# Key and query transposes of six batches moved from the tensor engine to the vector engine, with a larger feed-forward share in the first half

## The chip, the cores and the metric

The kernel runs on one core of one Trainium2 chip (trn2). The metric is the device time of one execution in microseconds, smaller is better; the kernel before was run three times and its median is given. The engines are named as the profile names them: PE is TensorE (PEld its weight loads), DVE VectorE, ACT ScalarE, POOL GpSimd, and SP the engine that issues most DMAs (SPq is its queue).

## What is computed

Top-k attention over 8 batches, 8 heads, 576 tokens and a head size of 64 is followed by a feed-forward layer with an ELU:

```python
scores = scale * np.matmul(q, k.transpose(0, 1, 3, 2))      # (8, 8, 576, 576)
kth = np.partition(scores, -32, axis=-1)[..., -32:-31]
scores = np.where(scores >= kth, scores, -1000000000.0)
attn = np.exp(scores - scores.max(-1, keepdims=True))
attn = attn / (attn.sum(-1, keepdims=True) + 1e-09)
x = np.matmul(attn, v)              # -> (4608 tokens, 512)
h = x @ w_in                        # (512, 2048)
g = np.where(h > 0.0, h, np.exp(np.minimum(h, 0.0)) - 1.0)
out = g @ w_out                     # (2048, 512)
```

The weights arrive as 64-bit floats, which the kernel turns into fp32 on the chip in its first steps. Everything else is fp32.

## The kernel before

*Steps.* The work is cut into 144 steps. Most steps are one pair of heads of one tile of 128 queries; the last 64 queries of a batch take two pairs in one step, so that a batch has 18 steps. A step goes through all engines. PE makes the scores (line 322) into PSUM, and ACT copies them out (line 342). DVE finds the 32nd largest score of each row in four rounds of MAX8 (lines 347 and 359), with three MATCH_REPLACE8 between them (line 353), for each of the two heads; these are nearly all of DVE's work. POOL turns the 32nd value into a mask (lines 371 to 373), ACT takes the exponential (line 409), PE transposes the result (line 449) and multiplies it with v (line 482). When all four pairs of a tile are through, DVE inverts the row sums (lines 418 to 420), SP sends them through DRAM to all partitions, and POOL normalises the tile (line 497).

*Feed-forward.* Normalised tiles are gathered into blocks of one to three. When the last tile of a block is normalised, the block's feed-forward is cut into pieces and put at the end of a list: 32 pieces of `hidden` (line 517, products with w_in) and 8 pieces of `project` for each tile (line 541, products with w_out). A piece has a cost in units written out by hand. In each step `feed` takes pieces off the list until a share of units is used up: the share is what is left, divided by the steps until the next block is due, but at most 6.0 in steps 0 to 71 and 7.2 after (line 580). What is still on the list after the last step is issued at the end. The list is what PE, ACT and POOL interleave with attention.

*Keys and queries.* There are 32 pairs of heads, p = 0 to 31, four a batch. For each, `load_qk` brings k and q to SBUF with tokens on the partitions, in four DMAs of 256-byte runs (one head's row of 64 values). `transpose_qk` turns them with PE: eight transposes of 128x128 (line 273) and two of the remaining 64 tokens (line 281) go to PSUM, and two ACT copies bring them to a buffer `kq` in SBUF (line 268). `keep_kq` stores it to DRAM in the next step (line 296), and `load_kq` loads it again for each step that uses it, once each odd step for the two steps that follow it, one step before their scores (line 302). The pool `kq` has five buffers, the pool `ld` for incoming k and q two.

*Order.* The order of the instructions is written out by hand, engine by engine in program order. Each engine works through its own instructions in that order, and SP also holds its DMA issues in that order, each behind the waits of the one before. Scores are made at even steps n for steps n + 2 and n + 3. The dictionary `turns` says at which step a pair is transposed: pairs 8 to 12 at steps 7 to 11, pair 13 at step 13, and from there every second step, up to pair 31 at step 49. This stands in the step behind the scores and ahead of the first MAX8, and `load_next` issues the loads of the next pair directly behind it. The functions that are touched, and the main loop that calls them, are these:

Of the kernel before, what the change touches and what calls it, by code (L numbers as in the profile page):

```python
# [61 lines left out]
def kernel(  # L62
# [150 lines left out]
    def load_qk(b, hp):  # L213

        first = b == 0 and hp < 2
        aside = (b, hp) in ((0, 1), (0, 2))
        if aside:
            home = xtpool.tile([P, 2, NC * T // 2], FP32, tag="xT", name="kqin")
            home = home[:, :, 0 : (J + 1) * 2 * D].rearrange(
                "p n (j h d) -> p n j h d", j=J + 1, h=2  # L220
            )
        for n, (name, src) in enumerate((("k", k), ("q", q))):
            queue = nc.scalar if first and name == "q" else nc.sync
            if aside:
                t = home[:, n]
            else:
                t = ldpool.tile([P, J + 1, 2, D], FP32, tag="in", name=name + "in")
            queue.dma_start(
                t[:, 0:J, :, :],
                src[b, 2 * hp : 2 * hp + 2, 0:JP, :].rearrange(  # L230
                    "h (p j) d -> p j h d", j=J
                ),
            )
            queue.dma_start(
                t[0:R, J, :, :],
                src[b, 2 * hp : 2 * hp + 2, JP:S, :].rearrange("h p d -> p h d"),
            )
            loaded[b, hp, name] = t

    def load_v(b, hp):  # L240

# [16 lines left out]
    def transpose_qk(b, hp, shared=False):  # L258

        t = kqT[b, hp] = kqpool.tile([P, 2, S], FP32, tag="kq", name="kq")  # L260
        src = [loaded.pop((b, hp, name)) for name in "kq"]

        def copy(at, ps):
            if shared:
                nc.scalar.copy(t[:, 0, at], ps[:, 0])
                nc.vector.tensor_copy(t[:, 1, at], ps[:, 1])
            else:
                nc.scalar.copy(t[:, :, at], ps)

        ps = ps_x.tile([P, 2, JP], FP32, tag="x", name="qkps")  # L270
        for n in range(2):
            for c in range(J):
                nc.tensor.transpose(  # L273
                    ps[:, n, c * P : (c + 1) * P],
                    src[n][:, c, :, :].rearrange("p h d -> p (h d)"),
                    ident[:],
                )
        copy(slice(0, JP), ps[:])
        ps = ps_x.tile([P, 2, JP], FP32, tag="x", name="qkps")
        for n in range(2):  # L280
            nc.tensor.transpose(
                ps[:, n, 0:R],
                src[n][0:R, J, :, :].rearrange("p h d -> p (h d)"),
                ident[0:R, 0:R],
            )
        copy(slice(JP, S), ps[:, :, 0:R])
# [287 lines left out]
    def feed(n, part):  # L574

        left = sum(piece[0] for piece in ffn)
        until = next(r for r in dues if r > n) - n
        share = min(left / until, 6.0 if n < NS // 2 else 7.2)  # L580

        work = 0.0
        for blk in order:
            mine = [piece[0] for piece in ffn if piece[3] is blk]
            work += sum(mine)
            late = work - 1.75 * 8 * blk.n
            if mine and late > 0 and blk.over is not None:
                share = max(share, late / max(blk.over.filled - n, 0.5))
        owed[0] = min(owed[0] + part * share, 8.0)
        while ffn and owed[0] > ffn[0][0] / 2 and ffn[0][2] < decoded[0]:  # L590
            t, piece = ffn.pop(0)[:2]
            piece()
            owed[0] -= t
# [37 lines left out]
    def sums(u):  # L631
        u.summed = True
        invert(u.g)
# [3 lines left out]
        if place in ((2, 3, 4, 5, 6) if n in (4, 5) else (3, 4, 5, 6)):  # L637
            weight_slot()

    todo, turns = {}, {}  # L640

    def at(step, fn, *args):
        todo.setdefault(step, []).append((fn, args))
# [2 lines left out]


    for p, pair in enumerate(pairs):
        if p >= NHP:
            n = p - 2 if p < NHP + 4 else p - 1  # L650
            n = n if n < EARLY + 5 else EARLY + 5 + 2 * (n - EARLY - 5)
            turns[n] = pair
            at(n + 1, keep_kq, *pair)
        elif p >= 2:
            at(p - 1, keep_kq, *pair)

# [13 lines left out]

    with tc.manual_schedule():
        load_qk(0, 0)
        nc.scalar.activation(rec[:], rec[:], AF.Copy)
        for hp in (1, 2):
            load_qk(0, hp)
        load_weights(3)
        warm(16)
        for hp in range(2):
            transpose_qk(0, hp, shared=hp == 0)
            steps[hp].kq = {hp: kqT[0, hp]}  # L680
            scores(steps[hp], 0)
            scores(steps[hp], 1, nc.vector.tensor_copy if hp == 0 else nc.scalar.copy)
            if hp == 0:
                load_qk(0, 3)
        load_weights()
        load_v(0, 0)
        first_max(steps[0])
        weight_slot()
        weight_slot()
        for hp in range(2):  # L690
            keep_kq(0, hp)
        for n in range(NS + 4):
            early = n < EARLY
            now, last, done = (
                steps[n + d] if 0 <= n + d < NS else None for d in (0, -1, -2)
            )
            for fn, args in todo.pop(n, []):
                fn(*args)
            gone = None
            if early:  # L700
                if n + 2 < NHP:
                    transpose_qk(0, n + 2)
                ahead = steps[n + 2]
                ahead.kq = {hp: kqT[0, hp] for hp in ahead.hps}
                for half in range(2):
                    scores(ahead, half)
                if n < EARLY - 1:
                    warm(24)
            elif n % 2 == 0:

                for d in (2, 3):
                    if n + d < NS:
                        for half in range(2):
                            scores(steps[n + d], half)
                    if d == 2:
                        for u in steps[n - 4 : n - 2]:
                            if not u.attended:
                                attend(u)
                                gone = u
            if n in turns and not early:  # L720
                transpose_qk(*turns[n])
                load_next()
            if now and n > 0:
                first_max(now)
            if last and n > EARLY:
                biases(last, early)
                mask(last, 0)
            if early:
                decode(n, 0)
                feed(n, 0.5)  # L730
                if last:
                    exp(last, 0)
                    exp(last, 1)
                next_max(now, (n, 1))
                decode(n, 2)
                if last:
                    trans(last)
                feed(n, 0.5)
                if last and last.ends:
                    sums(last)  # L740
                next_max(now, (n, 3))
                decode(n, 4)
                if last:
                    attend(last)
                if n in turns:
                    transpose_qk(*turns[n])
                if n < EARLY - 1:
                    warm(24)
                next_max(now, (n, 5))
                if last and last.ends:  # L750
                    normalise(last.g)
                mask_early(now)
                decode(n, 6)
                if n >= NHP - 3:
                    load_next()
                continue
            decode(n, 0)
            feed(n, (0.3, 0.7)[n % 2])
            if now:
                next_max(now, (n, 1))  # L760
            decode(n, 2)
            if last:
                if n > EARLY:
                    mask(last, 1)
                exp(last, 0)
            if done and not done.turned:
                trans(done)
            if now:
                next_max(now, (n, 3))
            decode(n, 4)  # L770
            if gone and gone.ends:
                normalise(gone.g)
            feed(n, (0.3, 0.7)[n % 2])
            if now:
                next_max(now, (n, 5))
            decode(n, 6)
            if last:
                exp(last, 1)
            if done and done.ends and not done.summed:
                sums(done)  # L780
        while ffn:
            ffn.pop(0)[1]()

# [32 lines left out]
```

## Time and profile before

| | |
|---|---|
| median of three runs | 1659.16 us (1658.2 to 1660.7) |
| the profiled execution's own time | 1660.85 us |
| its span in the profile | 1659.0 us |
| PE busy | 1593.8 us (96%) |
| DVE busy | 1460.3 us (88%) |
| POOL busy | 1141.9 us (69%) |
| ACT busy | 925.5 us (56%) |
| DMA: moved, mean rate | 174.53 MB, 105 GB/s |

The profile is one execution as the chip's profiler recorded it. The span is the time from the first to the last instruction on record; the execution's own time is a little longer. The page cuts the span into 40 slices and gives the busy tenths of each engine in each; a table of stretches gives the busy microseconds of each engine in any stretch of the span. A row of the groups has: line, engine, operation, what it writes and reads, shapes and count, then the total busy time, the mean duration of one in nanoseconds, and the idle time of the engine just ahead of it. A duration runs from the start of an instruction to its end, and neighbours on an engine overlap, so that the distance between starts can be shorter.

### The profile page before, as it was taken

The numbers are of one execution on the slowest core, as the hardware profiler recorded it, in microseconds if no ns is written. First come the engines' busy times: TensorE is split into PE (matmuls) and PEld (weight loads), VectorE is DVE, ScalarE is ACT, GpSimd is POOL, SyncE is SP. The second block draws the span as 40 slices with busy tenths as digits, with TensorE's granted clock in tenths as the row PEclk, the third lists the DMA queues.
The fourth block names the chain that finished last, engine by engine and source line by source line (L and its number), as shares of the span: only waits on it lengthen the run. The fifth ranks groups of instructions, "written<-read, shape, count | busy, mean of one in ns | idle before, by whom it ended". The sixth has DMA issues, their size and how long they took to land.

```text
span 1659.0 us, 28820 instructions
## 1 busy us (share of the span) xinstructions
PE 1593.8 (96%) x10048; PEld 1074.0 (65%) x10048; DVE 1460.3 (88%) x3074; ACT 925.5 (56%) x1889; POOL 1141.9 (69%) x1456
## 2 busy tenths in 40 slices
PE   6868999999999999999999999999999999999999
PEld 5765877777776776757566566566565566566565
DVE  6999999999999999999999989979989989987000
ACT  5875565656666565646466475466466466455121
POOL 3677777777777786868678678668668668668021
PEclk8879999999999999999999999999999999999999
DMA  9864555444543513121212321221212322210000
GB/s 304 266 184 120 185 186 152 141 132 134 162 141 97 187 52 104 65 88 67 85 71 102 116 83 61 77 85 65 91 70 100 113 68 82 77 42 7 26 7 13
DMA packets 138962, 174.53 MB, mean 105 GB/s; under 512 B 94272, under 2 KB 102464, under 8 KB 138816
## 3 DMA queue, kind: packets, MB, share of 16 engines
q1 hardware_dynamic: 136448, 172.09, 32.3%
q8 instruction: 80, 1.31, 0.3%
q10 hardware_dynamic: 2368, 0.59, 0.2%
q14 instruction: 66, 0.54, 0.1%
HBM read 144.18 MB, written 28.46 MB: 104 GB/s over the span
## 4 chain that ended last, share of the span: by engine, by line
PE 59%; DVE 26%; POOL 5%; issue 4%; DMA 3%; ACT 2%; SPq 1%; POOLq 0%; ACTq 0%
PE ops L541 21%; PE hps L517 19%; DVE m L359 11%; DVE wk L353 11%; PE avps L482 6%; PE scps L322 6%; PE eps L449 4%; DVE m L347 2%; POOL sc L373 1%; POOL gT L534 1%; DMA kin<-in_k_dram 1%; DMA w_out<-in_moe_w_in_dram 1%; POOL wk L371 1%; PE qkps L273 1%; POOL wk L372 1%
## 5 line engine op out<-in xcount | busy, mean ns | idle before, releaser
L359 DVE MAX8 m<-wk 128x8 f32<-128x576 f32 x864 | 609.8, 748 | 0.0
L517 PE MATMUL hps<-xT,w_in 128*128 128x128 f32 (+2 forms) x2432 | 534.6, 375 | 10.4 <-ACT gT L532 5.7
L541 PE MATMUL ops<-w_out,gT 128*128 128x512 f32 x1152 | 519.6, 597 | 7.6 <-ACT osb L550 7.6
L517 PEld LDWEIGHTS hps<-xT,w_in 128*128 128x128 f32 x2432 | 385.0, 194 | 134.8 <-issue 18.5
L353 DVE MATCH_REPLACE8 wk<-m,wk 128x576 f32<-128x576 f32 x576 | 423.6, 744 | 0.0
L373 POOL TENSOR_TENSOR sc<-sc,wk 128x576 f32<-128x576 f32 x276 | 389.2, 1410 | 23.0
L541 PEld LDWEIGHTS ops<-w_out,gT 128*128 128x128 f32 x1152 | 209.9, 190 | 240.2 <-issue 214.2
L409 ACT ACTIVATE sc<-sc,neg 128x576 f32<-128x576 f32 x288 | 224.1, 778 | 229.6 <-POOL sc L373 228.8
L534 POOL TENSOR_TENSOR gT<-gT,n 128x384 f32<-128x384 f32 (+1 forms) x168 | 187.2, 1121 | 189.7 <-ACT n L533 187.0
L371 POOL TENSOR_SCALAR wk<-sc,nth 128x576 f32<-128x576 f32 x276 | 206.2, 747 | 26.9
L353 DVE MATCH_REPLACE8 wk<-m,sc 128x576 f32<-128x576 f32 x288 | 211.8, 744 | 0.0
L342 ACT COPY sc<-scps 128x576 f32<-128x576 f32 x287 | 168.9, 639 | 75.6 <-PE scps L322 73.6
L322 PE MATMUL scps<-kq 64*128 64x288 f32 (+3 forms) x1344 | 181.3, 419 | 23.7 <-ACT sc L342 9.9
L347 DVE MAX8 m<-sc 128x8 f32<-128x576 f32 x288 | 201.3, 741 | 0.3
L372 POOL TENSOR_SCALAR wk<-wk 128x576 f32<-128x576 f32 x276 | 184.0, 667 | 22.8
L454 ACT COPY et<-eps 128x1024 f32<-128x1024 f32 x144 | 144.5, 1004 | 96.3 <-PE eps L449 95.3
L482 PE MATMUL avps<-et,vE 128*64 128x128 f32 (+1 forms) x3200 | 176.3, 265 | 5.6 <-ACT et L454 3.3
L482 PEld LDWEIGHTS avps<-et,vE 128*64 128x64 f32 x3200 | 158.7, 137 | 32.1 <-issue 24.7
L449 PEld LDWEIGHTS eps<-ident,sc 128*128 128x128 f32 x1152 | 134.1, 141 | 54.2 <-issue 36.6
L322 PEld LDWEIGHTS scps<-kq 64*128 64x128 f32 (+1 forms) x1344 | 101.5, 175 | 93.3 <-issue 31.2
L449 PE MATMUL eps<-ident,sc 128*128 128x128 f32 x1152 | 151.1, 274 | 7.3 <-ACT sc L409 4.6
L531 ACT ACTIVATE n<-hps 128x384 f32<-128x384 f32 (+1 forms) x168 | 90.2, 537 | 114.0 <-PE hps L517 105.4
(71 smaller groups left out, 1001.3 us busy)
## 6 DMA issues: line engine op xcount, KB each, us to landing
kq<-kqd SPq DMA_DIRECT2D x152, 576.0 KB
kqd<-kq SPq DMA_DIRECT2D x32, 576.0 KB
rb<-recd SPq DMA_DIRECT2D x64, 128.0 KB
out_dram<-osb SPq DMA_DIRECT2D x32, 256.0 KB
kin<-in_k_dram SPq DMA_DIRECT2D x30, 256.0 KB
qin<-in_q_dram SPq DMA_DIRECT2D x29, 256.0 KB
w_out<-in_moe_w_in_dram SPq DMA_DIRECT2D x2, 2048.0 KB
vE<-in_v_dram SPq DMA_DIRECT2D x32, 128.0 KB
```

The source lines that it names most:

```text
L322: nc.tensor.matmul(ps[rows, j, at : at + keys.stop - keys.start], u.kq[hp][r, 1, q0 : q0 + g.ql], u.kq[hp][r, 0, keys], start=True, stop=True,
L347: nc.vector.max(u.m1[:, i, :], u.sc[:, i, :])
L353: nc.vector.match_replace(u.wk[:, i, :], u.m[:, i, :], u.cur[:, i, :], TAKEN)
L359: nc.vector.max(u.m[:, i, :], u.cur[:, i, :])
L371: nc.gpsimd.tensor_scalar(pen, s, u.nth[:, i : i + 1], 2.0**100, ALU.add, ALU.mult)
L373: nc.gpsimd.tensor_tensor(s, s, pen, ALU.add)
L409: nc.scalar.activation(s, s, AF.Exp, bias=u.neg[:, i : i + 1], scale=scale, accum_out=g.den[:, at : at + 1],)
L449: nc.tensor.transpose(ps[:, i, c * P : (c + 1) * P], e[:, k0 + c * P : k0 + (c + 1) * P], ident[:],)
L482: nc.tensor.matmul(g.av[r, hp, 0:ql], vE[g.b, hp][:, i, (c + i) % (J + 1), :], u.et[:, at, q0 : q0 + ql], start=(c == 0), stop=(c == J),)
L517: nc.tensor.matmul(ps[:, f % G, :], w_in[:, i, f * P : (f + 1) * P], blk.xT[:, i, 0:N], start=(i == 0), stop=(i == NC - 1),)
L534: nc.gpsimd.tensor_tensor(g, g, n, ALU.subtract)
L541: nc.tensor.matmul(blk.o[:], blk.gT[f // NG][:, f % NG, s * P : (s + 1) * P], w_out[:, f, :], start=(f == 0), stop=(f == NF - 1),)
```

## The change

Pairs 0 to 7 (batches 0 and 1) stay as they are. For pairs 8 to 31 (batches 2 to 7) k and q are no longer loaded with tokens on the partitions. `load_blocks` loads each of them in eight DMAs, four for the first 512 tokens and four for the last 64, one for each group of 32 partitions: the group holds one half (32 values) of one head's row, and the runs are 128 bytes. The tokens are laid out so that, when each block of 32 partitions by 32 columns is transposed where it stands, the result is the layout of `kq`. `transpose_blocks` does that with one DVE instruction for k and one for q, each over 128 partitions and 576 columns, from the load buffer straight into `kq`.

The places move as well. A pair is transposed at the end of its step, at steps 13, 17, 21 and so on, every fourth step up to 105; k is loaded from the start of three steps ahead, q from the start of two steps ahead, and `keep_kq` follows one step behind. The call of `transpose_qk` and `load_next` in the later steps is gone. The upper limit of the share in steps 0 to 71 is 6.6 instead of 6.0.

```diff
--- before.py
+++ after.py
@@ -236,6 +236,32 @@
                 src[b, 2 * hp : 2 * hp + 2, JP:S, :].rearrange("h p d -> p h d"),
             )
             loaded[b, hp, name] = t
+
+    def load_blocks(b, hp, name):
+        t = ldpool.tile([P, J + 1, 2, D], FP32, tag="in", name=name + "bl")
+        t = t[:].rearrange("p j h d -> p (j h d)")[:, 0:S]
+        main = t[:, 0:JP].rearrange("p (c g d) -> p c g d", c=J, d=32)
+        rem = t[:, JP:S].rearrange("p (g d) -> p g d", d=32)
+        for part in range(4):
+            rows = slice(32 * part, 32 * part + 32)
+            h, d0 = 2 * hp + part // 2, part % 2 * 32
+            src = (k if name == "k" else q)[b, h, :, d0 : d0 + 32]
+            nc.sync.dma_start(
+                main[rows], src[0:JP].rearrange("(g i c) d -> i c g d", i=32, c=J)
+            )
+            nc.sync.dma_start(
+                rem[rows], src[JP:S].rearrange("(g i) d -> i g d", i=32)
+            )
+        loaded[b, hp, name] = t
+
+    def transpose_blocks(b, hp):
+        t = kqT[b, hp] = kqpool.tile([P, 2, S], FP32, tag="kq", name="kq")
+        for n, name in enumerate("kq"):
+            nc.vector.transpose(t[:, n, :], loaded.pop((b, hp, name)))
 
     def load_v(b, hp):
 
@@ -577,7 +603,7 @@
 
         left = sum(piece[0] for piece in ffn)
         until = next(r for r in dues if r > n) - n
-        share = min(left / until, 6.0 if n < NS // 2 else 7.2)
+        share = min(left / until, 6.6 if n < NS // 2 else 7.2)
 
         work = 0.0
         for blk in order:
@@ -637,7 +663,7 @@
         if place in ((2, 3, 4, 5, 6) if n in (4, 5) else (3, 4, 5, 6)):
             weight_slot()
 
-    todo, turns = {}, {}
+    todo, turns, blocks_at = {}, {}, {}
 
     def at(step, fn, *args):
         todo.setdefault(step, []).append((fn, args))
@@ -646,11 +672,15 @@
 
 
     for p, pair in enumerate(pairs):
-        if p >= NHP:
-            n = p - 2 if p < NHP + 4 else p - 1
-            n = n if n < EARLY + 5 else EARLY + 5 + 2 * (n - EARLY - 5)
-            turns[n] = pair
+        if p >= 2 * NHP:
+            n = EARLY + 7 + 4 * (p - 2 * NHP)
+            blocks_at[n] = pair
+            at(n - 3, load_blocks, *pair, "k")
+            at(n - 2, load_blocks, *pair, "q")
             at(n + 1, keep_kq, *pair)
+        elif p >= NHP:
+            turns[p - 2] = pair
+            at(p - 1, keep_kq, *pair)
         elif p >= 2:
             at(p - 1, keep_kq, *pair)
 
@@ -717,9 +747,6 @@
                             if not u.attended:
                                 attend(u)
                                 gone = u
-            if n in turns and not early:
-                transpose_qk(*turns[n])
-                load_next()
             if now and n > 0:
                 first_max(now)
             if last and n > EARLY:
@@ -778,6 +805,8 @@
                 exp(last, 1)
             if done and done.ends and not done.summed:
                 sums(done)
+            if n in blocks_at:
+                transpose_blocks(*blocks_at[n])
         while ffn:
             ffn.pop(0)[1]()
 
```

## Prediction

> **What bounds the kernel now.** I read the sliced rows of the page first: who is full, and where does it change?
>
> ```profile
> PE   6868999999999999999999999999999999999999
> DVE  6999999999999999999999989979989989987000
> ```
>
> PE and DVE are both full for most of the span, and DVE falls silent for the last three slices. So there are stages. I cut the span at the first MAX8 of a step on line 347 (144 steps, numbered from 0): step 12 starts at 186.7 us, step 72 at 780.1, step 84 at 901.4, the last DVE work ends at 1544.8. Busy time in these stretches (columns: PE, PEld, DVE, ACT, POOL, clock, DMA share, GB/s):
>
> ```profile
> 186.70:780.10 593.40, 581.63 (x4242) 427.36 (x4241) 592.08 (x1258) 356.52 (x714) 451.49 (x580) 1.00 0.39 122
> 780.10:901.40 121.30, 121.30 (x678) 76.31 (x677) 118.08 (x250) 73.47 (x157) 96.03 (x125) 1.00 0.25 87
> 901.40:1544.80 643.40, 633.10 (x3664) 381.75 (x3663) 580.60 (x1231) 352.10 (x756) 460.19 (x597) 1.00 0.22 74
> 1544.80:1659.00 114.20, 108.70 (x411) 67.61 (x409) 0.00 (x0) 22.14 (x41) 16.47 (x13) 0.99 0.04 14
> ```
>
> Steps 12 to 71: DVE idles 1.3 us of 593, 9.89 us a step; PE idles 12. DVE sets the pace, with PE just behind it. From step 84 on PE sets it: DVE idles 63 us of 643. The last 114 us are PE alone, on feed-forward left over. So time added on DVE before step 72 is paid in full, and PE work taken out from behind step 72 is gained in full.
>
> Who ends DVE's waits (waiter, releaser: total us, times, longest):
>
> ```profile
> DVE wk L353 <- POOL sc L373: 46.2, 16, 7.6
> PE scps L322 <- ACT kq L268: 7.6, 4, 5.1
> ```
>
> DVE waits for POOL's mask, which stands in POOL's queue among feed-forward results that come from PE: PE's lateness seen through POOL. The costs come from these groups:
>
> ```profile
> L359 DVE MAX8 m<-wk 128x8 f32<-128x576 f32 x864 | 609.8, 748 | 0.0
> L420 DVE STREAM_TRANSPOSE recT<-rec 128x32 f32<-128x32 f32 x40 | 8.5, 212 | 1.4
> ```
>
> and from a look at PE in one step (start, us, what):
>
> ```profile
> 440.26 0.66 PE L273 MATMUL qkps<-ident,kin 128*128 128x128 f32 x4
> ...
> 441.55 0.71 PE L517 MATMUL hps<-xT,w_in 128*128 128x128 f32 x4
> 442.09 3.60 PE L541 MATMUL ops<-w_out,gT 128*128 128x512 f32 x8
> 445.53 1.04 PE L449 MATMUL eps<-ident,sc 128*128 128x128 f32 x8
> ```
>
> One pair's ten transposes hold PE from 440.26 to 441.55, 1.29 us. Eight records of a 512-column product hold it from 442.09 to 445.53; the trace has two records for each fp32 product of the program (1152 for 576), so a product takes 0.86 us and one column 1.68 ns.
>
> [...]
>
> **The change, part by part.**
>
> *Transposes on DVE.* The built program has 48 new ones of 128x576, two a pair, at the end of steps 13, 17, ... 105. [...] neighbours overlap (MAX8 lasts 748 but starts every 660)[...]. Lower bound 0.66 (a MAX8's pace; a gain is excluded, DVE loses no work). [...] I take 0.69. Fifteen pairs (13 to 69) lie where DVE sets the pace: 30 x 0.69 = +20.7 us. The nine from 73 to 105 lie where DVE has idle time: 18 x 0.69 = 12.4 us against 18 us that DVE idles in steps 72 to 107. Their cover is thin; see the idle term.
>
> *Waits it adds.* Each transpose waits for eight DMAs, the first also for PE to be done with its kq buffer. Behind it on DVE stands the whole next step. The last block of q is issued from step n-2 on, so 28 us before use; loads issued shortly before use now land in time (PE waited 2.9 us in all for kin). I take 0; a late load costs its lateness, 0 to 3 us a pair.
>
> *Transposes off PE.* 240 transposes go, 24 x 1.29 = 31 us of PE, all of them in steps 7 to 49, where DVE sets the pace: worth nothing there by themselves. They make the room for the next part. The 24 pairs of ACT copies go too: ACT is 56% busy, nothing.
>
> *Share 6.6.* I followed the feed arithmetic through both programs and counted feed-forward columns. Steps 0 to 11: 20,992 before, 21,760 after. Steps 12 to 71: 200,192 and 215,808. Steps 72 to 147: 312,320 and 308,736. Emitted after the loop: 56,320 and 43,520. So 16,384 columns leave the part behind step 72: x 1.68 ns = -27.5 us. They go where PE then has: PE was busy 581.6 us in these 60 steps; less 19 pairs (24.5) and plus 15,616 columns (26.2) it is 583, 9.7 us a step against 10.2 of DVE. DVE is hiding them; were it not, PE would pay the 27.5 back.
>
> *The stall at step 12.* DVE waits 3.1 us at 188.1 us, at the end of a stretch where PE transposes a pair nearly each step. Five of these go (-6.5 us of PE) and 768 columns come (+1.3). I count -3.1; 0 is the other end.
>
> *New idle time of PE behind step 72.* Two sources. First, steps 72 to 107 (780 to 1154 us) held 371 us of PE and 356 of DVE; less 2048 columns (3.4) and plus 12.4 both stand at 368, so that PE runs out when it has a light step. Second, the store of pieces is thin: when block 12 becomes ready, 26.2 us of older pieces stood ahead of it, now 1.8 (blocks 11 to 16 alike, 1.8 to 3.5). PE comes to the new block about a step after its normalisation is emitted, and may wait for xT; at such thin stores in the early blocks it waited 4.7 us in two times. I take +4, from 0 to 15.
>
> *SP's queue.* 384 block issues take the place of 96; an issue of a k/q load held SP 0.62 to 0.71 us. Eight for q stand in front of the kq loads that PE's scores need one step later: 5.6 us. Where kq was issued 3.3 us before the scores PE did not wait, so it may come late by a few us; PE then lags, and the lag makes the next one on time. Nothing while DVE sets the pace; in the idle term's range otherwise.
>
> Sum against the profiled execution: 1659.0 + 20.7 - 27.5 - 3.1 + 4 = 1653.1 us of span. That execution took 1660.85, 1.85 more than its span, and lay 1.69 over the median of 1659.16. So 1653.1 + 1.85 - 1.69 = 1653.3.
>
> **The rivals.**
>
> *PE starves behind step 72* (no change). Thin stores, late kq loads and DVE's nine late pairs cost 12 us instead of 4: 1661.3. For it: six blocks with 2 us of store each. Against: PE lags DVE by some us in that stage, so that its inputs are ready.
>
> [...]
>
> *Blocks land late* (slower). Short runs and a blocked SP hold DVE at the transpose: 1 us a pair over 15 pairs is +15, 1668.3. It turns the sign from 0.4 us a pair. Against: 28 us of lead.
>
> *The change doesn't do what it says*: the columns do not move. The counts come from the built program, so I give it nothing.
>
> **How the numbers follow.** 0.2% is 3.3 us, about what a measurement of this kernel can tell from no change: faster is below 1655.8, slower above 1662.5. Forecast case 0.55 (its own range 1646 to 1657); PE starves 0.25; [...] late blocks 0.10. Faster is 0.55, the forecast case; no change 0.25, the starved one; slower 0.20. The low end takes 0.66 each (-0.9), no new idle (-4) and 2 us of lighter start: 1646. The high end reaches past the starved case with its full 15 us (1664) and the late blocks at 1668, to 1670[...].
>
> **What would show it.** Right: a wide transpose every 0.69 us; steps 13 to 71 near 10.2 us with DVE idle near 0; PE idle there up from 12 to some 28 us; DVE's end near 1560 and the part of PE alone some 20 us shorter. Wrong: [...] DVE waits for in_k or in_q ahead of them; PE waits for xT, kq or hps piling up behind step 72; the gap at 188 us still there.

## The result, and the profile after

The changed kernel takes 1698.4 us (median of four runs, 1697.29 to 1703.92) where the kernel before takes 1658.68 beside it: a ratio of 1.0246, 95% interval 1.022 to 1.0272. It is 40 us slower; the forecast was 1653.3, with a range of 1646 to 1670.

The same rows of the page as before, with the granted clock of PE below them:

```profile
PE   7867989989979989999889999999999999999999
...
DVE  7999999999979999999979998999999989989300
...
PEclk9988989999989999999999999999999999999999
```

PE has now 7s and 8s over the first half, where it had 9s, the clock drops in single slices, and DVE has single slices of 7 and 8 between its 9s. The last stretch of PE alone is shorter: two slices are empty of DVE instead of three.

Busy time by stage (columns: PE, PEld, DVE, ACT, POOL, clock, DMA share, GB/s), steps 12 to 71, 72 to 83, 84 to the last DVE work, and PE alone:

```profile
173.10:811.20 638.10, 588.61 (x4132) 428.28 (x4133) 613.72 (x1282) 340.36 (x685) 454.31 (x581) 0.97 0.37 110
811.20:943.60 132.40, 125.38 (x662) 77.03 (x659) 121.53 (x256) 69.95 (x149) 92.17 (x119) 0.96 0.32 97
943.60:1591.20 647.60, 631.74 (x3664) 380.84 (x3664) 602.25 (x1267) 356.49 (x763) 468.06 (x609) 1.00 0.28 87
1591.20:1695.50 104.30, 99.47 (x431) 65.07 (x429) 0.00 (x0) 23.32 (x43) 16.45 (x13) 1.00 0.05 15
```

In the first row both engines that could set the pace have room: DVE idles 24 us of 638, PE 49. Neither is the bound any more; they wait for each other, or both for a third. These are the waits that grew or are new:

```profile
DVE wk L379 <- POOL sc L399: 64.7, 22, 10.4
...
PE scps L348 <- DMA kq<-kqd: 51.5, 15, 9.0
...
PE hps L543 <- POOL xT L523: 8.7, 3, 6.5
```

PE waits 51.5 us, up to 9 at a time, for the loads of kq, a wait that the kernel before did not have at all. The transposes themselves are as priced, 0.68 us from start to start against the 0.69 taken:

```profile
L264 DVE STREAM_TRANSPOSE kq<-kbl 128x576 f32<-128x576 f32 x24 | 18.7, 779 | 4.6 <-issue 3.1 <-DMA recd<-recT 1.1 <-PE hps L543 0.2
...
L264 DVE STREAM_TRANSPOSE kq<-qbl 128x576 f32<-128x576 f32 x24 | 17.7, 736 | 0.0
```

Where the time went, by stage (a step starts with its first MAX8; microseconds on the profile's clock):

| stage | before | after | difference | two loads each (below) |
|---|---|---|---|---|
| up to step 12 | 175.5 | 173.1 | -2.4 | 175.6 |
| steps 12 to 71 | 593.4 | 638.1 | +44.7 | 618.3 |
| steps 72 to 107 | 373.6 | 392.6 | +19.0 | 377.1 |
| step 108 to DVE's end | 391.1 | 387.3 | -3.8 | 387.6 |
| PE alone | 125.3 | 104.3 | -21.0 | 104.3 |
| span | 1659.0 | 1695.5 | +36.5 | 1662.9 |

The span differs by 36.5 us where the medians differ by 40: of the kernel before a slower execution was profiled, of the changed kernel a faster one.

(In the prediction I had set the step times 11.2 us too late against the profile's clock: its first stretch should have begun at 175.5. The lengths of its first three stretches hold, but what lies in them shifts. Cut rightly, DVE idles 4.4 us of steps 12 to 71, not 1.3, since its wait of 3.1 us in step 12 falls inside; behind step 84 it idles 52 us, not 63; and PE works alone for 125.3 us, not 114.2. Which engine sets the pace in which stage stays the same, and no term of the sum changes.)

How a late kq load becomes a hold of DVE is seen in one place. SP's queue first (start, us, what):

```profile
448.31 1.55 SPq L450 DMA_DIRECT2D recd<-recT  x4
450.86 1.14 SPq L462 DMA_DIRECT2D rb<-recd  x2
452.09 0.54 SPq L322 DMA_DIRECT2D kqd<-kq  x1
452.68 0.62 SPq L252 DMA_DIRECT2D kbl<-in_k_dram  x1
...
458.49 0.78 SPq L277 DMA_DIRECT2D vE<-in_v_dram  x1
...
464.91 0.52 SPq L579 DMA_DIRECT2D out_dram<-osb  x1
465.79 0.64 SPq L252 DMA_DIRECT2D qbl<-in_q_dram  x1
...
471.07 2.04 SPq L328 DMA_DIRECT2D kq<-kqd  x4
```

From the moment recT lets it go, SP issues for 25 us with one pause of 1 us: the sums, eight blocks of k, ten pieces of v, an output, eight blocks of q, and only then kq. Sixteen of these 38 issues take the place of the four that a pair took before, and they hold SP for 10.3 us here. SP is not short of time on the whole: all its issues hold it for 286 us of the 638 of steps 12 to 71 (207 of 593 in the kernel before). But it waits in its order for recT, and what stands behind that wait comes in one burst. For the whole kernel that wait is

```profile
SPq L450 <- DVE recT L446: 535.9, 36, 37.9
```

Then the other engines:

```profile
475.01 2.29 PE L348 MATMUL scps<-kq 64*128 64x288 f32 x8 [8.98 <-DMA kq<-kqd]
...
486.17 1.27 POOL L560 TENSOR_TENSOR gT<-gT,n 128x512 f32<-128x512 f32 x1 [13.46 <-ACT n L559]
...
489.12 1.40 POOL L399 TENSOR_TENSOR sc<-sc,wk 128x576 f32<-128x576 f32 x1
...
490.55 0.09 DVE L379 MATCH_VALUE_LOAD wk<-m,sc 128x8 f32 x1 [10.45 <-POOL sc L399]
```

PE stands 8.98 us before the scores. From the issue of kq (471.07) to the scores (475.01) it took 3.9 us, so the issue came late, not the transfer. The scores themselves would not be missed for two steps, but PE's queue has a feed-forward piece behind them; POOL waits 13.46 us for that piece with the mask behind it, and DVE waits 10.45 us for the mask. The whole delay reaches DVE. And PE comes back at a lower clock (third row: 0.71, and in the row before 0.78, against 1.00):

```profile
455.00:465.00 10.00, 8.89 (x46) 7.88 (x46) 10.00 (x22) 4.85 (x11) 6.14 (x8) 1.00 0.39 85
465.00:475.00 10.00, 1.03 (x5) 0.59 (x4) 10.00 (x22) 2.40 (x6) 6.65 (x9) 0.78 0.56 153
475.00:485.00 10.00, 9.99 (x71) 8.12 (x72) 5.10 (x10) 2.97 (x6) 0.00 (x0) 0.71 0.36 148
485.00:495.00 10.00, 10.00 (x54) 8.92 (x53) 4.45 (x11) 6.28 (x15) 8.31 (x10) 1.00 0.01 2
```

### The profile page after: what moved, and what is told of

Read it like the earlier page. It is cut to its first block, busy times and chain, and to the rows that moved or that the text cites. A ratio compares the mean times of both kernels' runs of the same rounds, so it can differ in the third digit from the quotient of the medians.

```text
span 1695.5 us, 28732 instructions
## 1 busy us (share of the span) xinstructions
PE 1577.0 (93%) x9808; PEld 1057.2 (62%) x9808; DVE 1498.0 (88%) x3122; ACT 900.5 (53%) x1841; POOL 1141.0 (67%) x1456
## 4 chain that ended last, share of the span: by engine, by line
PE 50%; DVE 25%; POOL 7%; SPq 6%; issue 5%; DMA 4%; ACT 4%; DVEq 0%; POOLq 0%; ACTq 0%
PE ops L567 17%; PE hps L543 16%; DVE wk L379 10%; DVE m L385 10%; PE avps L508 7%; PE scps L348 6%; PE eps L475 4%; SPq L255 2%; DMA kq<-kqd 2%; SPq L252 2%; POOL sc L399 2%; DVE m L373 2%; POOL gT L560 2%; POOL wk L397 1%; POOL wk L398 1%
## 5 line engine op out<-in xcount | busy, mean ns | idle before, releaser
L348 PE MATMUL scps<-kq 64*128 64x288 f32 (+3 forms) x1344 | 191.0, 434 | 74.8 <-DMA kq<-kqd 51.5
L348 PEld LDWEIGHTS scps<-kq 64*128 64x128 f32 (+1 forms) x1344 | 106.9, 181 | 148.0 <-issue 77.1
L508 PE MATMUL avps<-et,vE 128*64 128x128 f32 (+1 forms) x3200 | 184.4, 273 | 5.6 <-ACT et L480 2.3
L508 PEld LDWEIGHTS avps<-et,vE 128*64 128x64 f32 x3200 | 166.8, 142 | 34.0 <-issue 26.1
L475 PEld LDWEIGHTS eps<-ident,sc 128*128 128x128 f32 x1152 | 133.2, 141 | 57.6 <-issue 36.5
```

The lines of the kernel that those rows point to most:

```text
L348: nc.tensor.matmul(ps[rows, j, at : at + keys.stop - keys.start], u.kq[hp][r, 1, q0 : q0 + g.ql], u.kq[hp][r, 0, keys], start=True, stop=True,
L475: nc.tensor.transpose(ps[:, i, c * P : (c + 1) * P], e[:, k0 + c * P : k0 + (c + 1) * P], ident[:],)
L508: nc.tensor.matmul(g.av[r, hp, 0:ql], vE[g.b, hp][:, i, (c + i) % (J + 1), :], u.et[:, at, q0 : q0 + ql], start=(c == 0), stop=(c == J),)
```

## The experiments

The theory, A: the time that SP needs to issue 384 block loads makes the kq loads late. The rivals: B, the share 6.6 leaves too thin a store of feed-forward pieces; C, the DVE transposes cost more than their own time; D, runs of 128 bytes are slow. Ratios are to the kernel before on the same chip, with 95% intervals.

**The share, alone and undone.** The changed kernel with 6.0, and the kernel before with 6.6.

```diff
-        share = min(left / until, 6.6 if n < NS // 2 else 7.2)
+        share = min(left / until, 6.0 if n < NS // 2 else 7.2)
```

> The changed kernel with the share of steps 0 to 71 back at 6.0; transposes and loads as changed. Theory A (SP's queue: sixteen block loads a pair stand in front of the kq loads, PE waits for kq, DVE is held later): PE still waits about 50 us for kq, and the 27.5 us of feed-forward go back behind step 72, while PE has more room to catch up; 1690 to 1710 us. Theory B (the thin store of feed-forward pieces starves PE): the store is thick again and PE's idle time behind step 72 falls back to about 12 us; 1659 + 21 for the transposes = about 1680 us.

Measured 1719.29 us, 1.0367 (1.0347 to 1.0386). PE still waits for kq, 64.7 us, and steps 12 to 71 take 638.7 us where they took 638.1: the thin store is not what holds them. B as the main cause falls; the time lies above A's range too. The share is worth 21 us to the changed kernel.

> The kernel before with the share 6.6 alone; PE still transposes. Theory A: nothing in the share itself hurts; PE, which idled 12 us in steps 12 to 71, is filled there (608 us of work in 593), those steps last about 15 us longer and the end part is 27.5 us shorter; about 1647 us. Theory B: the thin store costs 10 to 20 us of PE idle time behind step 72; 1660 to 1670 us.

Measured 1655.27 us, 0.9981 (0.9973 to 0.999): faster, but by 3 us and not by 12. Steps 12 to 71 took 611.4 us, 18 more (15 were expected), PE alone 21 less, and 2 us were lost in steps 72 to 107. So the share is a small gain by itself; a part of it is lost again where PE reaches a block before it is normalised (PE waited 6.9 us for xT in three times, 4.7 in two before).

**Fewer issues.** In the changed kernel k and q of a pair come in two DMAs each. This kernel leaves out the layout that the transposes need; it is there for its time.

```diff
-        for part in range(4):
-            ...
-            nc.sync.dma_start(main[rows], src[0:JP].rearrange(...))
-            nc.sync.dma_start(rem[rows], src[JP:S].rearrange(...))
+        src = (k if name == "k" else q)[b, 2 * hp : 2 * hp + 2]
+        nc.sync.dma_start(t[:, 0:JP]..., src[:, 0:JP].rearrange("h (p j) d -> p j h d", j=J))
+        nc.sync.dma_start(t[:, JP:S], src[0, JP - R : S])
```

> The changed kernel, but each of k and q comes in two DMAs with 256-byte runs instead of eight with 128-byte runs, in the layout of the kernel before; the blocks that DVE transposes then don't fall in place and the scores are of mixed values, all instructions but the loads are the same. Theory A: 96 issues instead of 384, the wait for kq falls from 51 us to under 10 us, DVE's holds shrink; about 1655 us. Theory C (the DVE transposes cost more than their own time): about 1690 us, since they stay. Theory B: also about 1690 us.

Measured 1661.52 us, 1.0017 (1.0008 to 1.0027). The wait for kq is down to

```profile
PE scps L344 <- DMA kq<-kqd: 4.5, 4, 3.1
```

and 37 of the 40 us are gone, with all 48 transposes in place: C falls as the main cause. The last column of the table above has its stages. It remains 8 us over the prediction's 1653.3.

**Issues against runs.** The last kernel changed two things, the number of issues and the length of the runs. So two more, each with one of them: eight issues with runs of 256 bytes, and two issues with runs of 128. Only the new lines are shown; they stand in place of the loads.

```diff
+        for part in range(4):
+            rows = slice(32 * part, 32 * part + 32)
+            nc.sync.dma_start(t[rows, 0:JP]..., src[:, 128 * part : 128 * part + 128].rearrange("h (p j) d -> p j h d", j=J))
+            nc.sync.dma_start(t[rows, JP:S], src[0, 32 * part : 32 * part + 32])
```

> The kernel with two loads each, its loads cut into eight of 32 partitions, still with 256-byte runs and the same bytes (mixed scores as there). Theory A (issue time on SP): as the changed kernel, 1690 to 1702 us. Rival D (short runs): as with two loads, 1661 us.

Measured 1697.73 us, 1.023 (1.0209 to 1.0251).

```profile
PE scps L346 <- DMA kq<-kqd: 54.0, 18, 9.4
```

```diff
+        src = (k if name == "k" else q)[b].rearrange("h s d -> (h s) d")[:, 0:32]
+        nc.sync.dma_start(t[:, 0:JP]..., src[0 : 16 * P].rearrange("(p r) d -> p r d", r=16))
+        nc.sync.dma_start(t[:, JP:S]..., src[16 * P : 18 * P].rearrange("(p r) d -> p r d", r=2))
```

> The kernel with two loads each, its loads in 128-byte runs as in the changed kernel (half of each of 2304 rows, 2304 packets a tensor; the values are of other rows and the scores are mixed). Theory A: as with two loads, 1660 to 1665 us. Rival D: near the changed kernel, 1690 us or more.

Measured 1663.8 us, 1.0031 (1.0019 to 1.0043).

```profile
PE scps L346 <- DMA kq<-kqd: 8.1, 5, 2.8
```

| | runs of 256 bytes | runs of 128 bytes |
|---|---|---|
| 2 issues a tensor | 1661.5 | 1663.8 |
| 8 issues a tensor | 1697.7 | 1698.4 |

The number of issues is worth 35 us, the length of the runs 1 to 2, which the intervals don't tell from nothing. D falls.

**The issues by themselves.** The kernel before, with 16 small DMAs a pair at the places of the blocks.

```diff
+    def idle_loads(b, hp, name):
+        t = scr.tile([P, 64], FP32, tag="scr", name="scr")
+        for part in range(4):
+            ...
+            nc.sync.dma_start(t[rows, 0:32], src[0:32, 0:32])
+            nc.sync.dma_start(t[rows, 32:64], src[JP : JP + 32, 0:32])
...
+            at(n - 3, idle_loads, *pair, "k")
+            at(n - 2, idle_loads, *pair, "q")
```

> The kernel before, with 16 more DMA issues at the places where the changed kernel loads the blocks of a pair (8 at n-3, 8 at n-2, n = 13, 17, ... 105), each of a 32x32 piece into a buffer that nobody reads; 384 issues, hardly any bytes, PE and DVE keep their work. Theory A (time that SP needs to issue): PE waits for kq for some 50 us in all as in the changed kernel, and PE has no room there; 1680 to 1700 us. Rival D (it is the short runs and their bytes, or the DVE's own part): no more than 1662 us.

Measured 1689.37 us, 1.018 (1.016 to 1.0199): 31 us for 384 issues that move 1.6 MB in all. They hold SP for 177 us. The wait for kq was 19.0 us, not 50, so a part of the loss is elsewhere: PE was also at half its clock for 26 us of steps 12 to 107, where the kernel before never was. How the loss divides between them is not shown. It lies in the same stages, +23 us in steps 12 to 71 and +7 in 72 to 107.

**The transposes by themselves.** The kernel before, with DVE transposes added.

```diff
+            if 13 <= n <= 105 and n % 4 == 1:
+                for _ in range(4):
+                    nc.vector.transpose(turned[:], w_in[:, 0, 0:288])
```

> The kernel before, with DVE transposes alone added at the places of the change: four of 128x288 at the end of steps 13, 17, ... 105, of a weight into a buffer that nobody reads; PE, loads and share as before. By the prediction's pricing 0.36 us each: 60 of them before step 72 are paid in full, 21.6 us, and those after lie in DVE's idle time; 1681 us, up to 1686 if they make PE wait there. Rival (a transpose holds DVE or POOL longer than its own time): 1695 us or more.

Measured 1685.83 us, 1.0159 (1.0142 to 1.0176).

```profile
L785 DVE STREAM_TRANSPOSE turned<-w_in 128x288 f32<-128x288 f32 x96 | 44.9, 468 | 2.5
```

All four write one buffer; they start 0.475 us apart, not the 0.36 of my estimate, and so, at 468 ns each, hardly overlap. Whether the one buffer is the reason was not tried. The 60 in steps 13 to 69 make 28.5 us, and steps 12 to 71 took 25.5 us longer, steps 72 to 107 only 1.9. DVE time is paid once where DVE sets the pace, and nearly nothing where PE does, as the prediction had it.

**Order on SP.** The kq loads of a step issued ahead of its blocks; then, besides, q's blocks one step later (n - 1 in the last line of the diff).

```diff
-            at(n - 3, load_blocks, *pair, "k")
-            at(n - 2, load_blocks, *pair, "q")
...
     for u in steps[EARLY + 2 :]:
         at(u.n // 2 * 2 - 3, load_kq, u)
+    for n, pair in blocks_at.items():
+        at(n - 3, load_blocks, *pair, "k")
+        at(n - 2, load_blocks, *pair, "q")
```

> The changed kernel with the kq loads of a step issued ahead of its block loads; nothing else. Theory A: kq is issued 5.3 us earlier in each step that loads q, so that the waits of up to 9 us shrink to about 3 to 4 us and most of the small ones go; 1665 to 1680 us. Theories B and C: no change, 1690 to 1700 us.

Measured 1668.34 us, 1.0057 (1.0035 to 1.0079). PE's wait for kq fell from 51.5 to 10.0 us, in six times, none over 3.1. Thirty of the 40 us go with nothing but an order, and the transposes, their loads and the share stay: A.

> The changed kernel with kq loads ahead of block loads, and q's blocks loaded at n-1 (an even step, in which no kq is loaded) instead of n-2. Theory A: no step has both a block load and a kq load, PE's wait for kq goes to nearly 0 and PE's clock no longer falls; about 1660 us, near the kernel with two loads each (1661.5). If the two-load kernel was better for its longer runs: like kq first, 1668 us.

Measured 1672.45 us, 1.0081 (1.0066 to 1.0096): not better, 4 us more, though the intervals touch. The wait for kq was 20.7 us in seven times. In front of the late kq loads stand, in two of the seven (7.6 us), q's blocks and pieces of v, and in the other five k's blocks and pieces of v; SP reached them late in its turn. A step of distance in the program is no distance in a queue that is behind.

**Another queue.** The blocks issued by ACT.

```diff
-            nc.sync.dma_start(main[rows], ...)
-            nc.sync.dma_start(rem[rows], ...)
+            nc.scalar.dma_start(main[rows], ...)
+            nc.scalar.dma_start(rem[rows], ...)
```

> The changed kernel with its 384 block loads issued by ACT instead of SP; layout, steps and order else as changed. Theory A: SP is free again, PE's wait for kq goes; ACT, busy 53%, takes 16 issues of 0.6 us in 40 us, but its queue now waits with the loads for DVE's transposes of the pair before; 1660 to 1670 us. If the wait for kq came from the DMA engines and not from SP's queue: 1690 us or more.

Measured 1869.76 us, 1.1264 (1.1235 to 1.1293), a clear miss. The wait for kq is gone, but each issue holds ACT itself, 388 for 233 us in all, and ACT's copies of the scores stand behind them, on which PE waits. Besides, ACT pauses between the issues of one tensor, 125 us in all, mostly until transfers of SP have landed by the trace; on SP the changed kernel has 1.4 us of such pauses. And half of the k loads, 12 of 24, begin only when DVE has ended the transposes of the pair before. So the 171 us over the changed kernel are not the price of the issues alone. The first of these waits and PE's:

```profile
ACT sc L368 <- DMA kbl<-in_k_dram: 178.6, 22, 12.3
...
PE scps L348 <- ACT sc L368: 155.7, 26, 11.6
```

**What is left of the 8 us.** The two-load kernel with the share 6.0.

> The kernel with two loads each (1661.5; blocks don't fall in place there, the scores are of mixed values) with the share back at 6.0. With SP out of the way this shows what the share is worth to the changed kernel. The prediction's sum: the 27.5 us come back behind step 72, less the 4 us it priced for the thin store, so 1685 us. If the thin store costs what the two-load kernel lies over the forecast (8 us more): 1677 us.

Measured 1678.26 us, 1.0115 (1.0098 to 1.0132). Its steps 12 to 71 took 610.8 us, 17.4 over the kernel before; with 6.6 they take 618.3. So the larger share costs the two-load kernel 7.5 us there, and is worth 17 us in all instead of 23.5. With 6.6 these steps have two waits of DVE for the mask, 3.3 us in step 13 and 5.0 in step 41; with 6.0 the longest is 0.9. Those two are about the 7.5 us. Waits in steps 12 to 71 of the two-load kernel with 6.6:

```profile
DVE wk L375 <- POOL sc L395: 8.2, 2, 5.0
PE hps L539 <- POOL xT L519: 2.6, 1, 2.6
```

PE's wait for xT grows from 8.8 us in two times to 16.6 in four, but only 2.6 us of that lie in these steps.

**A version.** Only the pairs of batches 6 and 7 go by DVE, at steps 77 to 105; the rest by PE as before, with kq ahead of blocks, q's blocks at n - 1 as in the last kernel of "Order on SP", and the share 6.6.

```diff
-        if p >= 2 * NHP:
+        if p >= 6 * NHP:
             n = EARLY + 7 + 4 * (p - 2 * NHP)
             blocks_at[n] = pair
-            at(n - 3, load_blocks, *pair, "k")
-            at(n - 2, load_blocks, *pair, "q")
             ...
         elif p >= NHP:
-            turns[p - 2] = pair
+            n = p - 2 if p < NHP + 4 else p - 1
+            n = n if n < EARLY + 5 else EARLY + 5 + 2 * (n - EARLY - 5)
+            turns[n] = pair
...
+    for n, pair in blocks_at.items():
+        at(n - 3, load_blocks, *pair, "k")
+        at(n - 1, load_blocks, *pair, "q")
...
+            if n in turns and not early:
+                transpose_qk(*turns[n])
+                load_next()
```

> A version: only the pairs of batches 6 and 7 go by DVE (steps 77 to 105), the rest by PE as before; kq loads ahead of block loads; share 6.6. DVE idled 18 us in steps 72 to 107 before and gets 11 us there; PE gets 10.3 us less than with share 6.6 alone (1655.3). Theory A: about 1646 us. If the issues hold PE in this stage too, where every us of PE counts, or PE's store of pieces is empty when it has room: 1655 to 1660 us.

Measured 1648.06 us, 0.9935 (0.992 to 0.995): faster than both kernels, and 7 us faster than the share alone. PE's wait for kq does not appear. Against the share alone the gain lies in steps 12 to 71, 601.6 us instead of 611.4: there PE sets the pace with 6.6, and the eight pairs that it no longer turns would stand in steps 35 to 49. Steps 72 to 107, where DVE turns them, take 1.4 us longer.

## Why the prediction was wrong

- **Price of a transpose: right.** 0.69 us was taken, my estimate: the kernel before has no transpose of this size on record. The starts are 702 and 659 ns apart, 0.68 us in the mean. The 30 before step 72 would have eaten the 26.6 us of the other terms (27.5 + 3.1 - 4) only from 0.89 us each on.
- **DVE's added time is paid in full before step 72: right.** 17.6 us were forecast for steps 12 to 71 (20.7 less the stall). With SP relieved and the share 6.0 it was 17.4: DVE worked 19.4 us more and waited 2.0 less. With transposes alone it was 25.5 of 28.5.
- **Columns taken from behind step 72: right for those after the loop.** PE alone lasts 21.0 us less (12,800 columns x 1.68 ns = 21.5). The other 3,584 columns, 6.0 us of the forecast 27.5, should have shortened steps 72 to the end of DVE. In the two-load kernel these steps last as long as before (+3.6 and -3.6), and PE idles 5.9 us more in them: the columns went, and new idle time took their place.
- **Waits for the blocks at the transpose: right.** DVE idled 4.6 us before all of them; "blocks land late" is out.
- **The stall at step 12: gone, with another in its place.** It was counted as gone, -3.1. In the changed kernel DVE does not wait in step 12, but 3.1 us in step 13. All nine kernels here with the share 6.6 have a wait of 2.1 to 3.3 us in step 13, and none of the five with 6.0 has; so it comes with the larger share. Nor was 3.1 a firm price: the kernel before with transposes added, the same program up to the end of step 13, waits 0.8 us in step 12.
- **New idle time of PE behind step 72: near; the share's price before it: left out.** 4 us were taken behind step 72, and the two-load kernel has 5.9. But the larger share also costs 7.5 us in steps 12 to 71 (two-load kernel with 6.6 against 6.0), where the prediction had no such term but DVE hiding the columns. What makes the two waits of DVE there is open. It is not the waits for xT alone, of which 2.6 us lie in these steps. The one in step 41 follows a wait of PE for kq of 3.1 us; with 6.0 PE waits 6.5 us for kq in step 39, and DVE loses nothing.
- **SP's queue: the step that failed.** The prediction saw the issues ("Eight for q stand in front of the kq loads that PE's scores need one step later: 5.6 us") and let them cost "Nothing while DVE sets the pace". They cost 35 us, in the profiles 20 in steps 12 to 71 and 15 in steps 72 to 107. Two things were wrong in it. It looked at the eight issues of q alone, at the distance seen in a quiet step; in the place shown above kq was issued 23 us after recT had let the queue go, with k's blocks and the loads of v in front as well. And it took a lag of PE for free while DVE sets the pace. What counted was what else waits on PE: the feed-forward piece behind the scores, and the mask behind that piece on POOL. Nor did "the lag makes the next one on time" hold: PE waited for kq in 15 places.

The sum by stage, on the profiled spans:

| stage | forecast | two loads each | changed kernel |
|---|---|---|---|
| up to step 12 | 0 | +0.1 | -2.4 |
| steps 12 to 71 | +17.6 | +24.8 | +44.7 |
| behind step 72 | -23.5 | -21.0 | -5.8 |
| span | 1653.1 | 1662.9 | 1695.5 |

With few issues the forecast misses by 9.8 us, 7.2 of them in steps 12 to 71; the profiled execution of that kernel was the slowest of its eleven, 3 us over its median. The rest, 32.6 us here and 35 to 37 in the medians, is the issues.

Not settled: how much of the 35 us is the wait itself and how much is PE's lower clock behind it. The clock was at one half for 51 us in steps 12 to 107 of the changed kernel, not once there in the kernel before, and for 20 us with two loads. No kernel took one without the other. The low clock by itself need not cost DVE anything: the two-load kernel with the share 6.0 was at half clock for 41 us of these steps, and its DVE idled only 2.4 us in steps 12 to 71. Not tried either: the sums in another place on SP, so that its queue doesn't stand behind recT.

## What to carry to other kernels

Each DMA issue held the queue it stood in, 0.62 us in the median for 8 KB of a block and 0.38 for the 576 KB of kq: count the issues of each step, add up the queue, and look for what the queue itself waits on, since what stood behind that wait came in one burst, 38 issues in 25 us; only then ask how long the bytes take. Where a change makes something late on an engine, follow what stands behind it there, and then on the next engine, rather than ask when its own result is needed: here 8.98 us of PE became 13.46 of POOL and 10.45 of DVE. Move work to a second full engine only in the stage where that engine has idle time: here added transposes cost 25.5 us for 28.5 us of work in steps 13 to 69, and 1.9 us for 17 us of work in steps 73 to 105.

## What the runs showed of the hardware

- The price of an issue did not follow the bytes. The median issue of a block held SP 0.58 to 0.61 us for 64 KB and 0.62 us for the remainder of 8 KB; the kq loads of 576 KB took 0.38, the added pieces of 4 KB 0.42. On ACT the blocks took as long (0.59 and 0.64), and the instruction behind them in ACT's order began only when the last was out: at 459.00 us, with the last issue from 458.32 to 458.96.
- VectorE's transpose of 128x576 fp32 lasted 779 ns for k and 736 for q, as long as a MAX8 of the same size (748).
- Runs of 128 bytes instead of 256, 2304 runs a tensor instead of 1152, cost 2.3 us with two issues a tensor (1663.8 against 1661.5) and 0.7 with eight (1698.4 against 1697.7), where the DMA engines were busy for 0.35 (two issues, long runs) and 0.37 (changed kernel) of steps 12 to 71. Halving the run hardly mattered here.
- In steps 12 to 107 of the changed kernel PE's granted clock fell to one half in gaps of PE of 3.1 to 9.0 us or just behind them, and came back 3.4 to 10.2 us after it fell, some of that time with PE at work again; a gap of 2.95 us left the clock alone. The other runs do not draw the line there. A gap of 2.3 us in the two-load kernel and one of 1.9 us in it with the share 6.0 brought 3.4 us at half clock, and one of 3.3 us in the kernel with two issues and short runs brought none.
